# Moving the attention visits of a fused attention + two-layer MLP + top-2 experts kernel to other half steps, and giving the second layer's four PSUM banks tiles of their own

## The chip, the cores and the metric

The kernel runs on one core of one Trainium2 chip. The metric is the device time of one execution in microseconds (us), lower is better. Five engines work side by side on one core: TensorE (PE in the profile, its weight loads PEld), VectorE (DVE), ScalarE (ACT), GpSimd (POOL) and SyncE (SP), the last one used here to issue DMAs. Each engine runs its own list of instructions strictly in the order in which the kernel's Python code emits them; semaphores order the engines among each other and are inserted by the framework from the tiles that an instruction reads and writes.

## The reference, cut to what matters

```
# 1. attention inside chunks of 64 rows, 8 batches x 8 heads x 576 rows x 64 columns
scores = q_c @ k_c.T / 8 ; attn = softmax(scores) ; x = attn @ v_c
x = x.transpose(0, 2, 1, 3).reshape(4608, 512)
# 2. an MLP, 512 -> 2048 -> 512
h = x @ w_in ; x = (h - tanh(h)) @ w_out
# 3. eight experts, two per token, 512 -> 1024 -> 512
noisy = x @ w_gate + log1p(exp(x @ w_noise)) * noise
top2, weights = two largest of noisy, softmax over the two
out[token] = sum over its two experts e of weight * (relu(x @ w1[e]) @ w2[e])
```

## The kernel before

The 4608 tokens are 36 tiles of 128. Eleven groups of 4, 3, 4, 3, 4, 3, 3, 3, 3, 3, 3 tiles (`GS`) go through the MLP, then the eight experts follow, three groups of token slots each. Group g of the MLP has 16 steps, one for each 128 columns of the hidden layer. A step is two blocks on PE: `layer1` (`products1`, line 269, 12 matmuls into the bank `hp`) and, one step later, `layer2` (`products2`, line 341, three matmuls for each tile, added up over the 16 steps in one PSUM bank of `accs` for each tile). Between the two, `activate` has ACT and DVE make the hidden values `gt`. After the last step of a group `store_y` (or `store_o` for the experts) copies the group's banks to SBUF, in turn on ACT and DVE (lines 383 and 385, 669 and 671).

**Half steps.** `advance(s, h)` emits the layer 1 block of a step, then what is listed in `slots[h]`, then the layer 2 block of the step before, then `slots[h + 1]`. So slot number h is a place in every engine's list right behind PE's block number h. A group of the MLP is `H1` = 32 half steps long. A half step of a group with 3 tiles takes PE about 2.1 us, one with 4 tiles about 2.8 us. All other work is put in these slots by `at(h, fn, ...)`; what is listed first in a slot is emitted first.

**Attention visits.** The attention of the tiles of group 0 is done in a prologue, that of the later tiles in visits, `u_attn`, each a piece of three tiles at once: the transposes of the softmax of the middle one (`u_t`), the product with V of the oldest (`p_mm`), the scores of the newest (`s_mm`), then `p_split` of the oldest (ACT and DVE read its product out of PSUM), and `s_max` and `s_sub` of the newest (DVE). The exponential (`u_x`, ACT) and the normalisation (`u_e`, DVE) of the newest follow one and two half steps later. A tile is finished after three visits. `s_mm(i)` and `p_mm(i)` also issue the loads of q, k and v of tile i + 2 on SP. The products of a visit are 64 small matmuls of 64 x 64, line 124, four at a time in quarters of the array. All of them write the tile `pair`, which has two PSUM banks.

**Other users of `pair`.** `misc()` hands out one of the two banks of `pair` to the logits (`u_lg`, line 415), the gates (`u_gate`, line 434) and the positions (`u_pos`, lines 516 and 517) of the group before; in group 0 `decode`, which turns 64 bit weights into 32 bit ones on DVE (lines 243 to 246), uses them too. The prologue's visits use, beside `pair`, the two halves of `accs`, which is one tile of four banks.

**What follows a group of the MLP.** In the next group, `u_z` (half steps 1 on) loads the stored rows again, `u_yt` (5 on, one each half step) transposes them on DVE (line 391), `u_lg` multiplies them with the gate weights at half step 9, or 10 where the group after this one has four tiles, `u_gate` comes two half steps later, `u_gate2` to `u_gate3` follow, `u_pos` comes 14 after `u_lg`. From there on the tokens are scattered: `u_pos` fills the list `waiting`, and `issue(s)`, called after each slot, pops one entry, a reload of a tile (then two indirect DMAs `xs`) or one indirect DMA `lst`, each behind a small POOL copy that waits for a mark of the step (line 318). The indirect DMAs are POOL instructions, line 544. With three tiles they are handed out from half step 23 to 31, with four into the first half steps of the next group.

**Where visits stand before.** Group 0: half steps 3, 8, 13, 21, 29. Later groups: 5, 13, 21, 29 where the next group has four tiles, else 11, 20, 29. The slot of a visit lists it ahead of everything else in that slot.

Of the kernel before, what the change touches and what calls it, by code (L numbers as in the profile page):

```python
# [9 lines left out]
F32 = mybir.dt.float32  # L10
# [7 lines left out]
PSUM = bass.MemoryType.PSUM  # L18
# [12 lines left out]
def moe_chain_kernel(ctx: ExitStack, tc: tile.TileContext, q, k, v, w_in, w_out, wgn, noise,  # L31
                     w1, w2, out):
    nc = tc.nc
    NT = q.shape[0]
    NTOK = NT * 128
    GS = SIZES or [4, 3] * 3 + [3] * ((NT - 21) // 3)
    NG = len(GS)
    G0 = [sum(GS[:g]) for g in range(NG)]
# [10 lines left out]
    pp = ctx.enter_context(tc.tile_pool(name="pp", bufs=1, space=PSUM))  # L49
# [8 lines left out]

    accs = pp.tile([128, 4, 512], F32, name="acc")
    pair = pp.tile([128, 2, 512], F32, name="pair")
    pairs = [accs[:, 0:2], accs[:, 2:4], pair]
    turn = {"acc": 0, "pair": 0, "early": 0}

    def after(what, n):
        turn[what] += 1
        return (turn[what] - 1) % n
# [126 lines left out]
        nc.scalar.copy(hi, px)  # L195
        nc.vector.tensor_tensor(lo, px, hi.bitcast(F32), op=ALU.subtract)  # L196

    def u_attn(i):

        old, mid, new = [t if GS[0] <= t < NT else None for t in (i - 2, i - 1, i)]  # L200
        for t, fn in ((mid, u_t), (old, p_mm), (new, s_mm), (old, p_split), (new, s_max),
                      (new, s_sub)):
            if t:
                fn(t)
# [139 lines left out]

    def new_acc(s):
        if s.f == 0:
            s.grp["acc"] = [accs[:, after("acc", 4)] for _ in s.tiles]

    def finish(s):
        if s.f == s.nf - 1:  # L350
# [2 lines left out]
    def layer2(s):  # L353
        new_acc(s)
        products2(s, len(s.tiles))
        finish(s)
# [408 lines left out]
    def step1(g, f):  # L765
        s = Step()
        s.kind, s.g, s.f, s.nf, s.n = 1, g, f, NF1, 128 * GS[g]
        s.tiles = [128] * GS[g]
        s.A, s.B, s.xt = WI, WO, XT[g]
        s.done = store_y  # L770
        return s
# [3 lines left out]
    def advance(s, h):  # L775
# [10 lines left out]
        if both:  # L786
            new_hp(s)
            new_acc(p)
            where_filled(s, lambda nt: (tail1(nt), tail2(nt)))
            activate(s)  # L790
            finish(p)
        elif s_tail:
            new_hp(s)
            where_filled(s, tail1)
            activate(s)
        elif s:
            layer1(s)
# [4 lines left out]
        if p_tail and not both:  # L802
            new_acc(p)
            where_filled(p, tail2)
            finish(p)
        elif p and not both:
            layer2(p)
# [6 lines left out]
    def L(f, *a):  # L814
        return lambda: f(*a)
# [11 lines left out]
    def decode_w(o, f, early=False):  # L827
        if f < NF1:
            RW[o, f] = decode(RW[o, f], early)
# [67 lines left out]
    rebias_w(1, 1)  # L897
    decode_w(0, 2)

    plans = [EVEN, ODD] if NG % 2 == 0 else [ODD, EVEN]  # L900
    g0 = plans[0][0]
    xt0, xts = {}, {}
# [9 lines left out]
    H1, H2 = 2 * NF1, 2 * NF2  # L912
    slots = [[] for _ in range(H1 * NG + H2 * E * 3 + 2)]

    def at(h, fn, *a):
        slots[h].append(L(fn, *a))

    values = {}
    for g in range(1, NG):
        for j in range(GS[g]):  # L920
            gap = 9 if GS[g] < 4 and g > 1 else 8
            values[G0[g] + j] = H1 * g - 3 - gap * (GS[g] - 1 - j)

    for i in range(GS[0], NT + 2):
        h = values.get(i - 2, 3 + 5 * (i - GS[0]))
        at(h, u_attn, i)
        if i < NT:
            at(h + 1, u_x, i)
            at(h + 2, u_e, i)

    for g in range(NG):
        h0 = H1 * g
        at(h0, load_nz, g)
        if g > 0:
            n = GS[g - 1]
            for j in range(n):
                i = G0[g - 1] + j
                at(h0 + 1 + j, u_z, i)
                at(h0 + 5 + j, u_yt, i)

            h = h0 + (10 if g + 1 < NG and GS[g + 1] > 3 else 9)
            at(h, u_lg, g - 1)
            h += 2
            for d, fn in zip((0, 2, 3, 4, 6, 7, 12), (u_gate, u_gate2, u_gate2a, u_gate2b,
                                                      u_gate2c, u_gate3, u_pos)):
                at(h + d, fn, g - 1)
        if g == 0:
            at(25, sums)
            at(26, store_consts)
            for f in range(NF1):  # L950
                at(2 * f, fetch_w, 0, f + 4)
                at(2 * f, decode_w, 1, f + 1)
                at(2 * f, prep_w, 0, f + 2)
                at(2 * f, rebias_w, 0, f + 3)
                at(2 * f + 1, fetch_w, 1, f + 4)
                at(2 * f + 1, decode_w, 0, f + 3)
                at(2 * f + 1, prep_w, 1, f + 1)
                at(2 * f + 1, rebias_w, 1, f + 2)
        else:
            for f in range(0, NF1):  # L960
                if g == 1:
                    if f < E:
                        at(h0 + 2 * f, zero_x, 2 * f)
                        at(h0 + 2 * f, zero_x, 2 * f + 1)
                elif (g - 2) * NF1 + f < NT + DUMMY // 128:
                    at(h0 + 2 * f, zero_out, (g - 2) * NF1 + f)
        if g == NG - 1:
            at(h0 - 4, u_cum)
            at(h0 - 2, u_bump)
            at(h0 + 12, load_list0)  # L970
            for c in range(min(3, SEAL // 128)):
                at(h0 + 8 + 3 * c, fetch_x, 0, c)
            for c in range(g0[1]):
                at(h0 + min(21 + 4 * c, H1 - 1), first_xt, c)
            for f in range(NF2):
                at(h0 + 2 * f + 7, fetch_e, 0, f)
                at(h0 + 2 * f + 10, prep_e, 0, f)
# [26 lines left out]
    for gi, (e, ge, c0, nt, n) in enumerate(groups):  # L1004
        h0 = H1 * NG + H2 * gi
        if gi == 0:
# [4 lines left out]
            h = h0 + 8 + GS[-1]  # L1011
# [18 lines left out]
    for g in range(NG):  # L1030
        grp = {}
        for f in range(NF1):
            s = step1(g, f)
# [3 lines left out]
    for gi, (e, ge, c0, nt, n) in enumerate(groups):  # L1037
        grp = {}
        for f in range(NF2):
            s = Step()  # L1040
# [60 lines left out]
```

## Time and profile before

| | |
|---|---|
| median of 3 runs | 1868.93 us (1867.94 to 1869.45) |
| the profiled execution | 1868.18 us, of which 1866.2 us are the span from its first to its last instruction |
| mean granted TensorE clock | 0.980 of full speed |
| MLP stage, about | 25 to 1003 us of the span; the last visit is at 926 us |
| experts, about | 1003 to 1855 us |

In the rows below, "[2.75 <-DVE e L144]" behind an instruction means that its engine sat idle for 2.75 us just before it, and that this ended with the DVE instruction of line 144 that writes `e`. "<-issue" means that it waited for nothing that the profile shows. L269 is line 269.

### The profile page before, as it was taken

The numbers are of one execution on the slowest core, as the hardware profiler recorded it, in microseconds if no ns is written. First come the engines' busy times: TensorE is split into PE (matmuls) and PEld (weight loads), VectorE is DVE, ScalarE is ACT, GpSimd is POOL, SyncE is SP. The second block draws the span as 40 slices with busy tenths as digits, with TensorE's granted clock in tenths as the row PEclk, the third lists the DMA queues.
The fourth block names the chain that finished last, engine by engine and source line by source line (L and its number), as shares of the span: only waits on it lengthen the run. The fifth ranks groups of instructions, "written<-read, shape, count | busy, mean of one in ns | idle before, by whom it ended". The sixth has DMA issues, their size and how long they took to land. (4 is left out here: it accounts for less than half of the span.)

```text
span 1866.2 us, 28364 instructions
## 1 busy us (share of the span) xinstructions
PE 1770.8 (95%) x10773; PEld 1511.3 (81%) x10775; DVE 802.1 (43%) x2064; ACT 546.7 (29%) x1105; POOL 490.9 (26%) x749
## 2 busy tenths in 40 slices
PE   6989999999999999998999999999999999999997
PEld 5768777887788888887888888888888888887886
DVE  7875434554344445353455442343334323333321
ACT  4543222332223222222233232232223222232211
POOL 3550303040304020211224532232232212322112
PEclk8999999999999999999999999999999999999999
DMA  6536343552213131222045343443434323433312
GB/s 253 197 107 159 108 102 109 151 153 75 86 63 123 41 111 52 86 74 74 36 125 168 106 109 84 108 96 78 113 73 101 96 58 81 103 98 78 67 23 34
DMA packets 197830, 184.68 MB, mean 99 GB/s; under 512 B 80176, under 2 KB 139568, under 8 KB 197680
## 3 DMA queue, kind: packets, MB, share of 16 engines
q1 hardware_dynamic: 178064, 142.73, 25.2%
q0 software_dynamic: 19328, 39.41, 10.6%
q8 instruction: 96, 1.57, 0.3%
q14 instruction: 54, 0.44, 0.1%
q10 hardware_dynamic: 288, 0.52, 0.1%
HBM read 118.76 MB, written 63.84 MB: 98 GB/s over the span
## 5 line engine op out<-in xcount | busy, mean ns | idle before, releaser
L269 PE MATMUL hp<-xt,wa 128*128 128x384 f32 (+3 forms) x4416 | 904.5, 354 | 1.2 <-ACT xt L195 0.7
L341 PE MATMUL acc<-wb,gt 128*128 128x512 f32 (+1 forms) x3510 | 882.6, 397 | 24.1 <-ACT o L669 10.4
L269 PEld LDWEIGHTS hp<-xt,wa 128*128 128x128 f32 x4416 | 785.8, 192 | 86.9 <-issue 3.1
L341 PEld LDWEIGHTS acc<-wb,gt 128*128 128x128 f32 (+1 forms) x3510 | 651.3, 188 | 168.9 <-ACT o L669 16.0
L300 DVE SCALAR_TENSOR_TENSOR gt<-hp,gt 128x384 fp32r<-128x384 f32 (+2 forms) x192 | 113.3, 590 | 451.0 <-ACT gt L297 438.2
L297 ACT ACTIVATE gt<-hp 128x384 fp32r<-128x384 f32 (+2 forms) x192 | 99.5, 518 | 455.9 <-PE hp L269 405.0
L292 DVE TENSOR_TENSOR g<-hp,g 128x384 f32<-128x384 f32 (+1 forms) x176 | 104.1, 591 | 257.6 <-ACT g L289 254.9
L289 ACT ACTIVATE g<-hp 128x384 f32<-128x384 f32 (+1 forms) x176 | 91.5, 520 | 356.2 <-PE hp L269 330.3
L254 POOL TENSOR_TENSOR wb<-st,wb 128x512 fp32r<-128x512 f32 x64 | 93.4, 1460 | 320.1 <-ACT wb L252 320.1
L318 POOL COPY spacer<-mark 1x1 f32<-1x1 f32 x182 | 45.8, 252 | 401.7 <-DVE mark L313 292.8
L293 ACT CAST gt<-g 128x384 fp32r<-128x384 f32 (+1 forms) x176 | 95.4, 542 | 160.0 <-DVE g L292 127.5
L674 POOL DMA_INDIRECT out_dram<-o,lsa x73 | 119.8, 1641 | 77.9 <-DVE o L671 59.1
L295 DVE TENSOR_TENSOR gt<-g,gt 128x384 fp32r<-128x384 f32 (+1 forms) x160 | 94.9, 593 | 96.1 <-ACT gt L293 87.4
L493 POOL TENSOR_SCALAR r<-d 128x3 f32<-128x3 f32 (+1 forms) x11 | 5.4, 487 | 406.5 <-ACT d L484 406.4
L544 POOL DMA_INDIRECT xs<-yr,row x72 | 71.5, 993 | 32.3 <-issue 25.3
L214 DVE TENSOR_TENSOR xt<-xg,xt 128x512 fp32r<-128x512 f32 x80 | 54.3, 679 | 54.4 <-ACT xt L213 54.4
L213 ACT CAST xt<-xg 128x512 fp32r<-128x512 f32 x80 | 48.8, 610 | 96.1 <-DVE xg L391 88.0
L544 POOL DMA_INDIRECT lst<-pay,row x72 | 70.6, 981 | 22.0 <-issue 21.1
L196 DVE TENSOR_TENSOR xt<-pair,xt 128x512 fp32r<-128x512 f32 x33 | 22.8, 691 | 89.6 <-ACT xt L195 79.7
L391 DVE STREAM_TRANSPOSE xg<-xg 128x512 f32<-128x512 f32 x80 | 56.4, 705 | 0.7 <-DMA xg<-xs 0.7
L124 PE MATMUL pair<-ks,q 64*64 64x64 f32 x1024 | 30.9, 226 | 21.7 <-issue 16.2
L671 DVE TENSOR_SCALAR o<-acc,lsa 128x512 f32<-128x512 f32 (+1 forms) x44 | 33.0, 750 | 39.2 <-PE acc L341 22.5
(194 smaller groups left out, 910.0 us busy)
## 6 DMA issues: line engine op xcount, KB each, us to landing
st<-in_w_dram SPq DMA_DIRECT2D x128, 256.0 KB
xg<-xs SPq DMA_DIRECT2D x320, 64.0 KB
out_dram<-zero SPq DMA_DIRECT2D x40, 256.0 KB
x2d<-y SPq DMA_DIRECT2D x36, 256.0 KB
z<-x2d SPq DMA_DIRECT2D x144, 64.0 KB
yr<-x2d SPq DMA_DIRECT2D x36, 256.0 KB
q<-in_q_dram SPq DMA_DIRECT2D x34, 256.0 KB
v<-in_v_dram SPq DMA_DIRECT2D x34, 256.0 KB
```

The lines of the kernel that those rows point to most:

```text
L254: eng.tensor_tensor(w[:, 1, :], x, w[:, 0, :].bitcast(F32), op=ALU.subtract)
L269: nc.tensor.matmul(s.hp[:, :m], lhsT=w[:, a, d, :], rhs=s.xt[:, b, d, :m], start=(i == 0), stop=(i == 11))
L289: nc.scalar.activation(g, hp[:, :n], AF.Tanh)
L292: nc.vector.tensor_tensor(g, hp[:, :n], g, op=ALU.subtract)
L293: nc.scalar.copy(hi, g)
L295: eng.tensor_tensor(lo, g, hi.bitcast(F32), op=ALU.subtract)
L297: nc.scalar.activation(hi, hp[:, :n], AF.Relu)
L300: nc.vector.scalar_tensor_tensor(lo, hp[:, :n], 0.0, hi.bitcast(F32), op0=ALU.max, op1=ALU.subtract)
L341: nc.tensor.matmul(s.grp["acc"][j][:m], lhsT=s.gt[:, a, j * 128:j * 128 + m], rhs=s.B[s.f][:, b, :], start=(s.f == 0 and i == 0), stop=(s. ...
L391: nc.vector.transpose(out=out.rearrange("p b (g c) -> p g b c", g=4), in_=x.rearrange("p (g b r) -> p g b r", g=4, b=4))
L544: s = nc.gpsimd.indirect_dma_start(out=to, out_offset=bass.IndirectOffsetOnAxis(ap=at, axis=0), in_=src, in_offset=None)
L674: a = nc.gpsimd.indirect_dma_start(out=out, out_offset=bass.IndirectOffsetOnAxis(ap=en[:m, 0:1], axis=0), in_=o[:m], in_offset=None, compu ...
```

## The change

The visits get half steps written out by hand: 3, 8, 13, 19, 25 in group 0, of which the last two take no new tile (so group 0 starts tiles 4 to 6 only, before it started 4 to 8); 2, 5, 9, 15, 18, 21 in group 1; later 5, 9, 15, 20 where the next group has four tiles, else 5, 14, 20, up to group 9. There are 36 visits in place of 34, with the same tiles. `u_lg` and all that hangs on it move from half step 10 to 11 where the next group has four tiles. The four banks of layer 2 are no longer slices of the one tile `accs`: the prologue has two tiles of two banks in a pool `ep`, which is closed after it, and the same four banks then become a ring of four tiles `acc` of one bank each.

```diff
-    accs = pp.tile([128, 4, 512], F32, name="acc")
     pair = pp.tile([128, 2, 512], F32, name="pair")
-    pairs = [accs[:, 0:2], accs[:, 2:4], pair]
-    turn = {"acc": 0, "pair": 0, "early": 0}
+    early = ExitStack()
+    ep = early.enter_context(tc.tile_pool(name="ep", bufs=1, space=PSUM))
+    pairs = [ep.tile([128, 2, 512], F32, name=f"pair{i}") for i in range(2)] + [pair]
+    turn = {"pair": 0, "early": 0}
+    accs = []
...
-    def u_attn(i):
-
-        old, mid, new = [t if GS[0] <= t < NT else None for t in (i - 2, i - 1, i)]
+    def u_attn(old, mid, new):
...
     def new_acc(s):
         if s.f == 0:
-            s.grp["acc"] = [accs[:, after("acc", 4)] for _ in s.tiles]
+            s.grp["acc"] = [accs[0].tile([128, 512], F32, name="acc", bufs=4) for _ in s.tiles]
...
+    early.close()
+    accs.append(ctx.enter_context(tc.tile_pool(name="ap", bufs=1, space=PSUM)))
...
-    values = {}
-    for g in range(1, NG):
-        for j in range(GS[g]):
-            gap = 9 if GS[g] < 4 and g > 1 else 8
-            values[G0[g] + j] = H1 * g - 3 - gap * (GS[g] - 1 - j)
-
-    for i in range(GS[0], NT + 2):
-        h = values.get(i - 2, 3 + 5 * (i - GS[0]))
-        at(h, u_attn, i)
-        if i < NT:
+    visits = [(3, 4), (8, 5), (13, 6), (19, None), (25, None)]
+    n0 = sum(GS[:2])
+    for g in range(1, NG - 1):
+        hs = (2, 5, 9, 15, 18, 21) if g == 1 else (5, 9, 15, 20) if GS[g + 1] > 3 else (5, 14, 20)
+        for h in hs:
+            visits.append((H1 * g + h, n0 if n0 < NT else None))
+            n0 += 1
+    flow = [None, None]
+    for h, i in visits:
+        at(h, u_attn, *flow, i)
+        if i:
             at(h + 1, u_x, i)
             at(h + 2, u_e, i)
+        flow = [flow[1], i]
...
-            h = h0 + (10 if g + 1 < NG and GS[g + 1] > 3 else 9)
+            h = h0 + (11 if g + 1 < NG and GS[g + 1] > 3 else 9)
             at(h, u_lg, g - 1)
```

## Rows read from the trace of the kernel before

**Rows 1.** Part 1 of the page: busy time of each engine, share of the span, instructions.
```profile
PE 1770.8 (95%) x10773; PEld 1511.3 (81%) x10775; DVE 802.1 (43%) x2064; ACT 546.7 (29%) x1105; POOL 490.9 (26%) x749
```

**Rows 2.** Who PE waited for over the whole span: the waiting instruction, what ended the wait, us in total, times, the longest.
```profile
PE pair L434 <- DVE e L144: 19.3, 7, 2.8
PE pair L124 <- issue: 16.2, 31, 1.1
PE pair L124 <- DVE x L246: 12.6, 5, 3.0
PE acc L341 <- ACT o L669: 10.4, 8, 2.2
...
PE acc L341 <- DVE o L671: 4.2, 7, 1.0
...
PE acc L341 <- ACT y L385: 3.4, 2, 2.7
PE acc L124 <- DVE xt L196: 2.3, 1, 2.3
PE acc L341 <- DVE y L383: 1.9, 3, 0.6
```

**Rows 3.** Timeline of PE at a visit with the gates in the same slot, group 8, half step 11: start, us, instruction.
```profile
799.07 0.94 PE L434 MATMUL pair<-summat,ls 128*128 128x16 f32 x6 [2.75 <-DVE e L144]
799.84 3.82 PE L269 MATMUL hp<-xt,wa 128*128 128x384 f32 x12
```

**Rows 4.** Stretches from the first matmul of line 124 of such a visit to the end of the next layer 1 block: window, us, busy us of PE (matmuls), of PEld, DVE, ACT, POOL, granted clock, share of the DMA engines, GB/s. The first, the second and the last of seven; the first two have blocks of 512 columns, the later ones of 384.
```profile
261.60:270.62 9.02, 6.27 (x83) 5.19 (x83) 2.16 (x4) 1.59 (x4) 0.00 (x0) 0.81 0.82 203
445.19:452.58 7.39, 4.64 (x83) 4.02 (x83) 2.16 (x4) 1.59 (x4) 0.00 (x0) 1.00 0.66 177
...
880.50:888.83 8.33, 5.58 (x83) 5.44 (x83) 2.17 (x4) 1.59 (x4) 0.00 (x0) 0.80 0.42 128
```

**Rows 5.** The same columns for stretches from the first matmul of line 124 of a visit to the end of the next layer 1 block, without gates in between. The first is in group 0 (blocks of 512 columns), the second at half step 5 of group 3 (384 columns). The other eight are the visits at half step 29 of groups 1 to 8; those that begin at 320.47 and 502.49 have 512 columns, the others 384.
```profile
76.45:80.41 3.96, 3.96 (x76) 3.39 (x77) 2.04 (x4) 1.77 (x4) 2.42 (x2) 1.00 0.54 155
344.08:347.35 3.27, 3.27 (x77) 3.20 (x77) 1.38 (x3) 1.17 (x2) 0.00 (x0) 1.00 0.62 160
213.81:224.28 10.47, 7.09 (x77) 5.89 (x77) 1.01 (x2) 1.17 (x2) 6.22 (x12) 0.77 0.53 184
320.47:326.61 6.14, 4.75 (x77) 3.78 (x77) 1.98 (x3) 1.17 (x2) 1.59 (x3) 1.00 0.34 98
401.90:405.78 3.88, 3.60 (x77) 3.41 (x77) 0.21 (x1) 1.17 (x2) 2.95 (x7) 1.00 0.69 247
502.49:510.37 7.88, 6.38 (x77) 5.15 (x77) 1.98 (x3) 1.17 (x2) 1.90 (x3) 0.78 0.30 102
588.55:591.84 3.29, 3.29 (x77) 3.22 (x77) 0.00 (x0) 0.59 (x1) 2.22 (x5) 1.00 0.66 212
670.74:680.78 10.04, 6.36 (x77) 5.60 (x77) 1.98 (x3) 1.18 (x2) 4.33 (x7) 0.83 0.34 107
756.16:766.13 9.97, 6.74 (x77) 5.39 (x77) 1.98 (x3) 1.17 (x2) 4.35 (x7) 0.83 0.27 86
841.64:851.56 9.92, 6.66 (x77) 5.33 (x77) 1.98 (x3) 1.18 (x2) 4.32 (x7) 0.83 0.17 55
```

**Rows 6.** Timeline inside the last of these visits, PE and POOL.
```profile
842.16 0.75 PE L124 MATMUL pair<-ks,q 64*64 64x64 f32 x13
...
842.86 0.97 POOL L544 DMA_INDIRECT lst<-pay,row   x1 [0.16 <-issue]
...
843.34 0.33 PE L124 MATMUL pair<-ks,q 64*64 64x64 f32 x4 [0.43 <-issue]
```

**Rows 7.** Timeline at the end of an expert's group of three tiles: the first two of three copies out of the layer 2 banks, and the first layer 2 block of the next group.
```profile
1192.53 0.75 DVE L671 TENSOR_SCALAR o<-acc,lsa 128x512 f32<-128x512 f32 x1 [1.07 <-PE acc L341]
1193.31 0.69 ACT L669 ACTIVATE o<-acc,lsa 128x512 f32<-128x512 f32 x1 [2.41 <-DVE o L671]
...
1194.93 1.86 PE L341 MATMUL acc<-wb,gt 128*128 128x512 f32 x7 [0.97 <-DVE o L671]
```

**Rows 8.** Timeline in the prologue: `p_mm(3)` on PE, which writes the second half of `accs` (`p_split(2)`, which it waits for, reads the first half); the last reader of `accs` in the prologue; the first layer 2 block.
```profile
23.62 1.13 PE L124 MATMUL acc<-pts,wb 64*64 64x64 f32 x32 [2.28 <-DVE xt L196]
...
25.43 0.69 DVE L196 TENSOR_TENSOR xt<-acc,xt 128x512 fp32r<-128x512 f32 x1 [1.87 <-ACT xt L195]
...
33.96 2.25 PE L341 MATMUL acc<-wb,gt 128*128 128x512 f32 x9
```

**Rows 9.** Timeline around a visit at half step 20 of group 8 (a visit at an even half step): the block of PE that follows it, and the last DVE instruction of `u_e`, which makes the softmax that the next visit transposes.
```profile
821.95 2.35 PE L341 MATMUL acc<-wb,gt 128*128 128x512 f32 x9
...
829.80 0.69 DVE L168 TENSOR_TENSOR e<-e,sm 128x512 f32<-128x512 f32 x1
```

**Rows 10.** Timeline in group 5, whose `u_lg` takes four tiles: the logits on PE and the last of the four transposes on DVE.
```profile
535.82 1.34 PE L415 MATMUL pair<-x2t,wg 128*32 128x128 f32 x32
...
535.97 0.71 DVE L391 STREAM_TRANSPOSE x2t<-z 128x512 f32<-128x512 f32 x1
```

**Rows 11.** A stretch at the visit at half step 5 of group 1, with the columns of rows 4.
```profile
155.99:160.00 4.01, 4.01 (x81) 3.81 (x81) 2.13 (x4) 1.67 (x3) 0.00 (x0) 1.00 0.86 213
```

**Rows 12.** Timeline of the end: the first of the last three copies out of the layer 2 banks, and the first of the last three indirect DMAs.
```profile
1855.30 0.75 DVE L671 TENSOR_SCALAR o<-acc,lsa 128x512 f32<-128x512 f32 x1 [2.45 <-PE acc L341]
...
1856.46 1.55 POOL L674 DMA_INDIRECT out_dram<-o,lsa  x1 [24.24 <-DVE o L671]
```

## The prediction

> **What bounds the kernel now.** First the busy shares: PE has 1770.8 us of matmuls in a span of 1866.2, every other engine is below half [rows 1]. So PE sets the time, and a change that adds no matmul work can only move what PE loses: idle time, and blocks that run at the slow one of its two clock levels. Second, PE's waits by cause [rows 2]: 19.3 us are seven waits of the gates for `s_sub` of a visit, 16.2 are gaps inside visits that end with no event ("issue"), 12.6 are visits behind a weight decode in group 0, and 19.9 (10.4 + 4.2 + 3.4 + 1.9) are layer 2 blocks that wait until the last group's banks are copied out. Third, stretches of equal work laid beside each other [rows 4, 5], which catch what the list of waits doesn't: the slow clock and matmuls that trickle.
>
> The sum is made against the profiled execution, 1868.18 us, which is the span plus 1.98 us; the median of the runs is 0.75 above it.
>
> **Gates.** At half step 11 a visit and `u_gate` share a slot and the tile `pair`. PE reaches the gates right behind the visit and stands 2.75 us until DVE has done `p_split`, `s_max` and `s_sub`; the next layer 1 block then takes 3.66 us (799.84 to 803.50) [rows 3]. The second of the seven stretches ran at full clock throughout and lost nothing but the wait: 7.39 - 2.75 = 4.64 us quiet for 512 columns [rows 4]. For 384 columns the quiet value is 0.69 less (3.96 against 3.27 in the two quiet visits of [rows 5]), 3.95. The losses are 9.02 - 4.64 = 4.38, then 2.75, then five of 8.33 - 3.95 = 4.38 (the one with four tiles differs by 0.2): 29.0 us. The granted means of 0.81 and 0.80 in the first and the last [rows 4] say that after the wait part of the stretch ran at 1.2 GHz. After the change the nearest user of `pair` behind a visit is two half steps away (visit 9, logits 11), 4.2 us against the 2.75 that DVE needs. So **-29.0**; bounds 25 and 29.
>
> **Visits among indirect DMAs.** The eight visits at half step 29 with the next block [rows 5] took 10.47, 6.14, 3.88, 7.88, 3.29, 10.04, 9.97 and 9.92 us; quiet is 3.27, or 3.96 where the block has 512 columns. Excess: 7.20 + 2.18 + 0.61 + 3.92 + 0.02 + 6.77 + 6.70 + 6.65 = 34.0 us. Inside the last one PE runs 13 score matmuls, then four in a burst, with gaps, while POOL issues one indirect DMA after another [rows 6]. No semaphore of the profile explains the gaps; what differs from the quiet visit is POOL's load (4.32 us busy against 0.00) [rows 5]. The case against: the fifth of the eight, with POOL busy for 2.22 us, lost nothing. With three tiles the indirect DMAs are over by half step 31, and the new places 5, 14, 20 are clear of them; with four tiles the last is popped at half step 4, so the visits at 5 of groups 2 and 4 stand just behind it. I take **-34.0** and, for these two, +2; bounds 0 and -34, and 0 to +14 (two at the worst price, 6.8).
>
> The Trainium skill says otherwise: "PE and ACT never wait on anyone" (SBUF — State Buffer, Who interferes with whom), meaning contention for SBUF's ports. By that rule POOL's DMAs can't be what held PE up, moving the visits would free nothing, and the sum would be 34 us higher. The eight stretches disagree about the waiting, six of them clearly, though not about the ports.
>
> **The ring of layer 2 banks.** At an expert group's end the copies run one behind the other though they read different banks: DVE 1192.53 to 1193.28, ACT from 1193.31, and the next group's layer 2 block starts at 1194.93 behind the third [rows 7]. That group has three tiles and the ring four banks, so the bank it writes first was free long before: the wait hangs on the tile `accs`, not on the bank. The prologue shows the same: `p_mm(3)` waits 2.28 us for a reader of the other half [rows 8]. With a tile for each bank, the copy of tile j starts when its own matmuls end (the last step is sorted by tile), ACT and DVE run side by side, and PE needs the first bank alone. Of the 19.9 us I take **-18**; two stay, because the longest wait for `y`, 2.7 us [rows 2], is more than three serial copies explain. Bounds 0 (the waits stay as they are) and -19.9. Closing the prologue's pool costs nothing: the first layer 2 block comes at 33.96, the last reader of those banks is done at 26.12 [rows 8]. The prologue's wait of 2.28 goes, and much of it reaches the first block: **-2**, bounds 0 and -2.3. At the end the first of three copies waits for the last matmul (idle 2.45 before it), and POOL's three DMAs follow it [rows 12]: **-1.5**, bounds 0 and -2.4.
>
> **Group 0.** Five visits before and after; the last two are smaller, but each still stands behind a decode on `pair`, so the 12.6 us stay: **0**, bounds 0 and -5 (two mean waits of 2.5).
>
> **What is late next: group 1.** It now has six visits, some three half steps (6.3 us) apart. After a visit at an even half step the softmax is ready at 830.49, which is 8.54 us after PE went on at 821.95 [rows 9]. So the visits at 5 and 21 wait 2.2 us each, in `u_t`, and all of PE behind them. The one at 18, behind an odd half step, has up to one DVE queue's work less: 1.2. That is 5.6 us, and a wait of 2.75 cost a slow block of 1.6 in six of seven cases [rows 4]; two such make 3.2. SP gets three loads more for each of the visits at 2 and 9, where at half step 5 the DMA engines are already 0.86 busy [rows 11]. In sum **+9**, bounds 0 and 20.
>
> **Logits.** In groups 2 and 4 to 9 a visit now stands at half step 5, ahead of the transposes that `u_lg` needs. It puts five DVE instructions of 0.69 us [rows 9] before the last of them, 3.5 us. In group 5, with four tiles, the last transpose already ends at 536.68, inside the logits' own 1.34 us [rows 10]: there PE waits about 2.5, and with a chance of a slow block 3.3. The other six have one transpose less, or longer half steps, and I give four of them 0.2 each. **+4**, bounds 0 and 7 x (3.5 + 1.6) = 36.
>
> No instruction is added on any engine but what two more slots hold; the q, k and v loads on SP are the same ones, moved. The half step by which `u_lg` and the scatters of groups 1 and 3 move later delays the reuse of `y` buffers; it is part of the two us left above.
>
> Sum: -29.0 - 34.0 - 18 - 2 - 1.5 + 2 + 9 + 4 = -69.5; 1868.2 - 69.5 = 1798.7, with the 0.75 of the median 1799.
>
> **The rivals.**
> A. PE isn't held up by the indirect DMAs, and visits trickle wherever they stand. For it: the visit of 3.29 us among them. Against: no visit away from half step 29 trickled in rows 5, at 0.62 DMA share. Time: 1799 + 34 = 1833. Chance 0.11.
> B. The framework orders the ring's tiles as it did the slices; the copies stay serial and PE waits for all. Against: the waits follow the tile in both [rows 7, 8]. Time: 1799 + 18 + 2 + 1.5 = 1820. Chance 0.10.
> C. The dense visits and the transposes cost their upper bounds rather than what I gave: DVE's list is late in group 1, and the logits wait in most groups. 1799 + 11 + about half of the 32 = 1826. Chance 0.13.
> D. Slower than before: visits at 5 run among the loads of `u_z` and starve as those at 29 did, 6.8 us each. From 11 starved visits of 36 on (69.5 / 6.8 = 10.2) the kernel is slower; twelve give 1799 + 82 = 1881. Against: the visits at half step 5 of groups 1 and 3 ran quiet among such loads [rows 5, 11]. Chance 0.04.
> E. None of the new costs shows: 1784. Chance 0.02.
>
> **How the numbers follow.** My forecast holds 0.60, own range 1786 to 1812. The range 1783 to 1826 leaves out A, D and a part of C, some 0.19. A difference of 0.2%, 3.7 us, is about what a measurement of this kernel can tell from none. All cases but D are faster by more than that; 0.02 I keep for no change, as a mixture of A, B and C: faster 0.94, same 0.02, slower 0.04.
>
> **What would show it.** Right: no wait of line 434 for `e`; no "issue" gaps at line 124; DVE and ACT copies of one group overlapping, and the waits of line 341 for `o` and `y` below 3 us together; new waits of line 178 for `e` of line 168 at three places in group 1; one of line 415 in group 5; a mean granted clock of 0.985 or more. Wrong: trickling line 124 at the new half steps (A, D), serial copies (B), or line 178 and 415 above 20 us (C).

## The result, and the profile after

On the chip where the kernel before took 1869.19 us (median of 4 runs), the changed one takes **1784.43 us** (median of 4 runs, 1783.46 to 1787.84): ratio 0.9549, 95% interval 0.9532 to 0.9565. The forecast was 1799 (1783 to 1826): the direction was right, and the gain of 84.8 us is 14.6 more than the 70.2 from that same median to 1799. The profiled execution took 1784.29 us, span 1782.4 after 1866.2.

Later runs fell on other chips and brought what no trace of before could show. On chip 11 (numbers as the results give them) the unchanged kernel before takes 1830.76 us, the changed one 1777.56: ratio 0.9713, interval 0.9698 to 0.9728. On chips 3 and 4 the kernel before takes 1863.81 and 1871.01. (The number of the first chip was not kept; it is called the first chip here.) About 39 of the 84 us between the two spans are a loss that the kernel before doesn't have on chip 11; the gain there is only 31 us smaller, because the changed kernel takes 7.6 us less there too.

Part 1 of the page after; it answers to [rows 1]. PE has 30.7 us less of busy time for the same 10773 matmuls: part of the time of trickling visits and of slow blocks counts as busy.

```profile
PE 1740.1 (98%) x10773; PEld 1492.3 (84%) x10775; DVE 796.6 (45%) x2064; ACT 546.4 (31%) x1105; POOL 491.8 (28%) x749
```

Who PE waited for in the changed kernel: the waiting instruction, what ended the wait, us in total, times, the longest; to be laid beside [rows 2].

```profile
PE pair L126 <- DVE x L246: 11.1, 5, 3.8
PE pt L180 <- DVE e L170: 4.7, 2, 2.7
PE pt L180 <- POOL e L170: 4.1, 2, 2.5
PE pt L180 <- DVE ef L500: 2.1, 1, 2.1
...
PE acc L341 <- issue: 1.5, 1, 1.5
...
PE pair L415 <- DVE x2t L391: 0.9, 2, 0.8
...
PE acc L341 <- ACT y L385: 0.5, 1, 0.5
```

Line 434 is gone, the gaps inside visits are gone, and of the layer 2 blocks' waits for `o` and `y` (19.9 us) 0.5 is left. The wait for the decode stays, and waits of line 180 (178 before) are new in group 1, as forecast; the two of them for POOL stand in the prologue, as before.

Timeline at the end of an expert's group of three tiles in the changed kernel, the answer to [rows 7]: the copies on DVE and ACT, and the blocks on PE.

```profile
1122.86 0.74 DVE L671 TENSOR_SCALAR o<-acc,lsa 128x512 f32<-128x512 f32 x1
1123.30 0.69 ACT L669 ACTIVATE o<-acc,lsa 128x512 f32<-128x512 f32 x1 [0.92 <-PE acc L341]
1123.80 1.63 PE L269 MATMUL hp<-xt,wa 128*128 128x352 f32 x12
...
1124.00 0.75 DVE L671 TENSOR_SCALAR o<-acc,lsa 128x512 f32<-128x512 f32 x1 [0.40 <-PE acc L341]
1125.27 1.79 PE L341 MATMUL acc<-wb,gt 128*128 128x512 f32 x7
```

DVE and ACT overlap (1123.30 lies inside 1122.86 to 1123.60), each copy starts when its own tile's matmuls are done, and line 341 starts without a wait.

Stretches of the changed kernel from the first matmul of a visit to the end of the next block on PE (columns of [rows 4]): the visits of group 6 at 5 and 20 (after the latter the block is one of layer 2).

```profile
583.00:586.29 3.29, 3.29 (x77) 3.22 (x77) 1.41 (x3) 1.17 (x2) 0.00 (x0) 1.00 0.37 112
...
619.67:622.93 3.26, 3.26 (x74) 2.83 (x74) 2.08 (x5) 1.65 (x4) 0.85 (x5) 1.00 0.44 143
```

Both are quiet: full clock, busy time equal to the stretch.

Where the time went, by the starts of the groups' first layer 1 blocks in the timelines (us; each column is one span less another):

| stretch | after less before, first chip | after less before, chip 11 | before: chip 11 less first chip |
|---|---|---|---|
| up to the first layer 1 block | -2.8 | -3.8 | +0.5 |
| group 0 | -5.6 | -6.7 | +0.7 |
| group 1 | +3.5 | +9.1 | -8.0 |
| groups 2, 3 | -6.6, -0.3 | -5.7, +0.3 | -0.9, -0.6 |
| groups 4, 5 | -9.6, -5.0 | -4.4, -4.6 | -5.3, -0.5 |
| groups 6, 7, 8 | -12.4, -11.3, -10.6 | -4.5, -4.5, -4.5 | -9.6, -6.7, -6.6 |
| groups 9, 10 | -4.5, +0.6 | -4.6, -0.3 | 0.0, +0.1 |
| experts | -18.7 | -17.7 | -2.1 |
| tail | -0.5 | -0.9 | +0.5 |
| sum | -83.8 | -52.8 | -38.6 |

The last column is the same program on two chips. Nearly all of its difference, 38.4 of 38.6 us, lies in groups 1 to 8, whose visits at half step 29 stand among the indirect DMAs [rows 5]. Elsewhere the start, group 0 and the tail differ by 0.5 to 0.7 the other way, the first three expert groups by 2.1; from the fourth expert group to the tail the two agree within 0.1 us.

### The profile page after: what moved, and what is told of

The parts are those of the page before. It is cut to its first block, busy times and chain, and to the rows that moved or that the text cites. A ratio compares the mean times of both kernels' runs of the same rounds, so it can differ in the third digit from the quotient of the medians.

```text
span 1782.4 us, 28350 instructions
## 1 busy us (share of the span) xinstructions
PE 1740.1 (98%) x10773; PEld 1492.3 (84%) x10775; DVE 796.6 (45%) x2064; ACT 546.4 (31%) x1105; POOL 491.8 (28%) x749
## 3 DMA queue, kind: packets, MB, share of 16 engines
q0 software_dynamic: 19328, 39.41, 11.1%
## 5 line engine op out<-in xcount | busy, mean ns | idle before, releaser
L269 PE MATMUL hp<-xt,wa 128*128 128x384 f32 (+3 forms) x4416 | 888.8, 350 | 1.4 <-ACT xt L197 1.4
L269 PEld LDWEIGHTS hp<-xt,wa 128*128 128x128 f32 x4416 | 771.2, 189 | 85.0 <-issue 2.2
L544 POOL DMA_INDIRECT xs<-yr,row x72 | 71.5, 993 | 31.3 <-issue 25.4
L254 DVE TENSOR_TENSOR wa<-st,wa 128x512 fp32r<-128x512 f32 x64 | 45.2, 706 | 7.5 <-ACT wa L252 7.4
L252 ACT CAST wa<-st 128x512 fp32r<-128x512 f32 x64 | 39.2, 613 | 6.6 <-DMA st<-in_w_dram 6.6
```

What stands on the lines that cost most here:

```text
L254: eng.tensor_tensor(w[:, 1, :], x, w[:, 0, :].bitcast(F32), op=ALU.subtract)
L269: nc.tensor.matmul(s.hp[:, :m], lhsT=w[:, a, d, :], rhs=s.xt[:, b, d, :m], start=(i == 0), stop=(i == 11))
L544: s = nc.gpsimd.indirect_dma_start(out=to, out_offset=bass.IndirectOffsetOnAxis(ap=at, axis=0), in_=src, in_offset=None)
```

## The experiments

**The ring alone.** The kernel before with the tiles of the layer 2 banks changed as in the change (the first and third hunk and the two lines after the prologue), visits where they were.

> The kernel before with the ring of layer 2 banks and the pool of the prologue alone; all visits where they stood before. My theory (the waits of the layer 2 blocks hang on the one tile of four banks): the experts lose 18.7 us as they do in the changed kernel, the waits for the copies of y in the MLP 5 to 6, the prologue 2.8, the tail 0.5, so 1841 to 1847 us (my sum gave this part 21.5: 1847). The trickling visits and the waits of line 434 stay as long as they were. Rival B (the framework orders the ring as it did the slices): 1869, with serial copies.

Measured on chip 11: 1803.78 us beside 1830.71, ratio 0.9856 (0.9839 to 0.9873): -26.9. My 1841 to 1847 were worked out from 1869, and this chip's level is 38 lower; the difference is the 22 to 28 expected. PE's waits in it (two lines were added ahead, so 434 is 436 here):

```profile
PE pair L436 <- DVE e L146: 19.3, 7, 2.8
PE pair L126 <- DVE x L248: 13.4, 5, 3.8
...
PE acc L343 <- DVE o L673: 0.2, 1, 0.2
```

The gates' 19.3 us are untouched, the waits for `o` and `y` are gone. Rival B falls. A line that should be there is missing: no "issue" gaps in visits, though they stand at half step 29 as before. The run of the unchanged kernel before, below, shows that this goes with the chip.

**The visits alone.** The changed kernel with the four banks as slices of one tile.

```diff
+    accs = pp.tile([128, 4, 512], F32, name="acc")
...
-    pairs = [ep.tile([128, 2, 512], F32, name=f"pair{i}") for i in range(2)] + [pair]
...
+    pairs = [accs[:, 0:2], accs[:, 2:4], pair]
...
-            s.grp["acc"] = [accs[0].tile([128, 512], F32, name="acc", bufs=4) for _ in s.tiles]
+            s.grp["acc"] = [accs[:, after("acc", 4)] for _ in s.tiles]
```

> The changed kernel with the four layer 2 banks as slices of one tile again; the visits at their new half steps. My theory: it gives back what the ring brought, 22 to 28 us, so 1806 to 1812 us, with waits of line 341 for o and y of some 20 us in the list. If the two parts don't add up (the ring also feeds the visits, or the visits hide the ring), it differs from 1869 + 1784 less the time of the ring alone by more than 5. Rival B: 1784.

Measured on chip 11: 1804.77 us, 27.2 above the changed kernel there (1777.56). PE's waits:

```profile
PE acc L339 <- ACT o L667: 11.5, 8, 3.3
...
PE acc L339 <- DVE o L669: 4.2, 7, 1.0
```

The waits for `o` and `y` are back (line 341 is 339 here; those for `y` are 1.3 us). The two halves add up: 26.9 for the ring, 25.9 for the visits (1830.71 - 1804.77), 53.2 for both on that chip. Neither feeds the other beyond some tenths.

**The last visit among the indirect DMAs again.**

```diff
-        hs = (2, 5, 9, 15, 18, 21) if g == 1 else (5, 9, 15, 20) if GS[g + 1] > 3 else (5, 14, 20)
+        hs = (2, 5, 9, 15, 18, 21) if g == 1 else (5, 9, 15, 29) if GS[g + 1] > 3 else (5, 14, 29)
```

> The changed kernel with the last visit of groups 2 to 9 at half step 29 in place of 20, among the indirect DMAs again; all other visits and the ring stay. My theory (a visit trickles where indirect DMAs run): the excess of rows 5 comes back where it was, 2.2 + 0.6 + 3.9 + 0 + 6.8 + 6.7 + 6.65 for groups 2 to 8, so some 27 us: 1811 (1804 to 1816). In group 9, whose last visit does not meet a later one, none. Rival A (the trickle had to do with the neighbours of the visit, not with the indirect DMAs): 1784, and no gaps that end with no event in line 126.

Measured on chip 11: 1781.17 us, 3.6 above the changed kernel there, 2.6 of them in group 1, where the two kernels are the same. The 1811 that I expected did not come; by the words on record this is rival A: no trickle. Stretches from those visits to the end of the next layer 1 block, groups 2 and 7:

```profile
311.03:314.99 3.96, 3.96 (x77) 3.39 (x77) 1.82 (x3) 1.17 (x2) 1.56 (x3) 1.00 0.48 142
...
711.34:714.60 3.26, 3.26 (x77) 3.19 (x77) 1.38 (x3) 1.17 (x2) 2.94 (x5) 1.00 0.60 208
```

POOL is 1.56 to 2.97 us busy in the seven stretches, with indirect DMAs, and nothing is lost. But the kernel before, run beside it, took 1830.71, not 1869. Before believing the rival, the kernel before itself had to be looked at on this chip.

**The kernel before once more**, unchanged.

> The kernel before once more. On the chip of the runs of the ring alone and of the visits at 29 it took 1830.7 us, 38 less than in the runs that I predicted from. My theory now: what is missing there are the 34 us of the visits that trickle among indirect DMAs (rows 5), so the loss belongs to some chips and not to the kernel alone. If this run takes 1867 to 1871, the visits at half step 29 trickle as in rows 5; if 1827 to 1832, all of them take 1.1 to 1.2 us, and the waits of line 434 for e (19.3), of line 341 for o and y (some 20) and for the decode (12.6) are as in rows 2. Rival: the 38 us lie elsewhere, in a higher granted clock or in shorter waits.

Measured on chip 11: 1829.59 us (one run). Four of the eight stretches of [rows 5], the same visits of the same program (groups 1, 4, 6, 8):

```profile
215.12:218.39 3.27, 3.27 (x77) 3.20 (x77) 1.27 (x2) 1.17 (x2) 2.84 (x6) 1.00 0.82 271
...
492.78:496.74 3.96, 3.96 (x77) 3.39 (x77) 1.98 (x3) 1.17 (x2) 1.91 (x3) 1.00 0.45 151
...
653.75:657.04 3.29, 3.29 (x77) 3.22 (x77) 1.29 (x2) 1.17 (x2) 2.96 (x5) 1.00 0.63 213
...
811.16:814.45 3.29, 3.29 (x77) 3.22 (x77) 1.29 (x2) 1.17 (x2) 2.97 (x5) 1.00 0.49 165
```

Quiet to the hundredth: 3.27 where [rows 5] has 10.47, 3.96 for 7.88, 3.29 for 10.04, 3.29 for 9.92. The other waits are nearly the same (gates 19.3 us, line 341 for `o` 9.8 + 4.2), but for one: the 3.4 us of line 341 for ACT's copies of `y` [rows 2] are not listed at all. POOL's side is the same: the 72 indirect DMAs into `lst` have a median of 967 ns, on the first chip 966. So the trickle is not in the program alone.

**The changed kernel once more**, unchanged.

> The changed kernel once more, beside the others of this call. My theory: it loses nothing to trickling visits on any chip, so 1778 to 1785 us wherever it runs, and its gain over the kernel before is 84 us on a chip where visits trickle and 46 to 52 on one where they don't. Rival (the other chip is quicker as a whole): it is 38 us quicker there too, 1746.

Measured beside it on chip 11: 1777.56 us (1776.71 to 1780.23), -53.2. As expected it is nearly the same on both chips; of the 7.6 us between the two spans 2.5 lie in group 1, 1.8 in group 6 (one "issue" wait of line 341, 1.48 us, at 576.52 on the first chip), the rest in pieces of about 1.

**The middle visit back beside the gates.**

```diff
-        hs = (2, 5, 9, 15, 18, 21) if g == 1 else (5, 9, 15, 20) if GS[g + 1] > 3 else (5, 14, 20)
+        hs = (2, 5, 9, 15, 18, 21) if g == 1 else (5, 9, 15, 20) if GS[g + 1] > 3 else (5, 11, 20)
```

> The changed kernel with the middle visit at half step 11 in place of 14 in the groups that had it at 14, so that it shares a slot with the gates and with the tile pair again. My theory: in each group in which a visit with new scores meets the gates there, 4.4 us (2.75 of wait for DVE and 1.6 of slow clock behind it), seven or fewer of them: 1784 + 22 to 31 = 1806 to 1815. Where only the wait comes back and no slow clock, 1784 + 2.75 x 7 = 1803. A rival: DVE's list is shorter than before and the wait shrinks to 1 or below: 1791 or less.

Measured on chip 11: 1811.73 us, 34.2 above the changed kernel there. By group: 4.4 in group 2, 6.0 and 5.8 in groups 4 and 5, 4.4 in each of 6 to 8, 1.5 in group 9, together 30.8; the rest is mostly group 1 (2.5 us of slow blocks), where this kernel does the same as the changed one. PE's waits, and the gates of one group (the wait, then the layer 1 block that follows):

```profile
PE pair L434 <- DVE e L146: 16.5, 6, 2.8
...
PE pair L434 <- DVE xt L198: 1.4, 1, 1.4
```
```profile
616.38 0.84 PE L434 MATMUL pair<-summat,ls 128*128 128x16 f32 x6 [2.76 <-DVE e L146]
617.07 3.64 PE L269 MATMUL hp<-xt,wa 128*128 128x384 f32 x12
```

The wait and a slow block come back with the place (2.76 and 3.64 here, 2.75 and 3.82 in [rows 3]). The gates' term holds.

**Without the indirect DMAs into `lst`.** The kernel before with a small POOL memset in the place of each, groups 0 to 8.

```diff
-                waiting.append(L(scatter, lst, row[:, 1, c:c + 1], pay[:, j, kk, :], "entries"))
+                if g >= NG - 2:
+                    waiting.append(L(scatter, lst, row[:, 1, c:c + 1], pay[:, j, kk, :], "entries"))
+                else:
+                    waiting.append(L(nc.gpsimd.memset, spacer, 0.0))
```

> The kernel before without the indirect DMAs that write the list entries (lst) of groups 0 to 8, a small POOL memset in the place of each; it leaves out that scatter, so most tokens are missing in the output. On a chip where visits trickle: the five visits of rows 5 that met lst (3.9 + 2.2 + 6.8 + 6.7 + 6.65 = 26 us) run quiet, 1843, and those that met xs (213.81 and 401.90) stay as they were; by rival A 1869. On a chip where they don't: 1827 to 1832, no change.

Measured on chip 11: 1831.65 beside 1830.76, ratio 1.0006 (0.9996 to 1.0016): nothing to gain where nothing trickles. Later the same kernel ran on chip 4:

> The kernel before without the indirect DMAs that write lst in groups 0 to 8 once more, in the hope of a chip on which visits trickle (it leaves out that scatter, so most tokens are missing in the output). If the kernel before takes 1860 to 1870 beside it: by my theory the visits at half step 29 that met lst, of groups 2, 4, 6, 7 and 8 (26 us in rows 5), run quiet, so 24 to 30 us less than the kernel before, while those of groups 1 and 3 that met xs trickle on. Rival (the transfers of q, k and v or POOL's marks hold PE up, not the indirect DMAs): within 3 us of the kernel before. If the kernel before takes 1830 it tells nothing new.

Measured there: 1842.44 us beside 1871.01, ratio 0.9847 (0.9813 to 0.9881): -28.6. The stretches that answer to [rows 5], groups 1 to 6 (7 and 8 are as 6, 3.27 and 3.29):

```profile
213.55:224.44 10.89, 7.31 (x78) 6.11 (x78) 1.98 (x3) 1.17 (x2) 5.33 (x12) 0.70 0.65 198
319.86:323.82 3.96, 3.96 (x77) 3.39 (x77) 1.98 (x3) 1.17 (x2) 0.05 (x1) 1.00 0.52 170
399.14:403.02 3.88, 3.58 (x77) 3.38 (x77) 0.00 (x0) 0.69 (x2) 2.96 (x7) 1.00 0.71 248
499.85:503.81 3.96, 3.96 (x77) 3.38 (x77) 1.98 (x3) 1.17 (x2) 0.06 (x1) 1.00 0.52 170
583.35:586.96 3.61, 3.47 (x77) 3.20 (x77) 0.00 (x0) 0.58 (x1) 2.55 (x8) 1.00 0.65 225
664.60:667.89 3.29, 3.29 (x77) 3.22 (x77) 1.41 (x3) 1.17 (x2) 0.61 (x5) 1.00 0.62 211
```

The five that had met `lst` are quiet now; the three that meet `xs`, left in place, are not (10.89, 3.88, 3.61). Same half step, same loads of q, k and v, same POOL copies: what went is the indirect DMAs. On a chip that shows the trickle they cause it; whether it is POOL's instruction or the transfer that it starts, this run doesn't separate.

**The last visit at 29 on a chip that trickles.** The kernel of the last experiment below (five tiles in group 0), with and without the visit at 29 in place of 20; its edit is the one that put the last visit at 29 above.

> The same with the last visit of groups 2 to 9 at half step 29 in place of 20, among the indirect DMAs. On a chip where the kernel before takes 1830 us and no visit trickles: the same time within 2 us (the visits at 29 cost nothing there, as in the first run of that place). On a chip where it takes 1869: 25 to 30 us more than the same kernel with that visit at 20, in visits of 3 to 7 us at half step 29.

Measured on chip 3: 1812.26 us, with that visit at 20 it is 1780.94: +31.3. The stretch of group 8:

```profile
810.00:820.37 10.37, 7.13 (x78) 5.88 (x78) 1.98 (x3) 1.18 (x2) 4.34 (x7) 0.74 0.17 53
```

The same edit that cost nothing at half step 29 on chip 11 costs 31.3 us here, the 25 to 30 that I expected and a little more. Over all seven stretches the excess is 27.0 us; the groups themselves lose 31.1: some 4 us fall after the next layer 1 block, outside the window that I had measured. In group 5, for one, PE waits 1.59 us for ACT behind it.

**Six visits in group 1 spread out.**

```diff
-        hs = (2, 5, 9, 15, 18, 21) if g == 1 else (5, 9, 15, 20) if GS[g + 1] > 3 else (5, 14, 20)
+        hs = (1, 5, 9, 15, 19, 23) if g == 1 else (5, 9, 15, 20) if GS[g + 1] > 3 else (5, 14, 20)
```

> The changed kernel with the six visits of group 1 at half steps 1, 5, 9, 15, 19, 23 in place of 2, 5, 9, 15, 18, 21, so that each has four half steps or more before the next. My theory: the three waits of line 180 in group 1 (2.05, 2.70, 2.14) and the slow blocks behind them go, 7 to 10 us less than the changed kernel: 1775 where that takes 1784. Rival (DVE's list is late for another reason, or the visit at 23 meets the first indirect DMAs): no change within 2 us.

Measured on chip 11: 1770.96 us (1769.54 to 1773.03), 6.6 below the changed kernel beside it. Line 180's waits for DVE in group 1 fall from 7.4 us (the changed kernel on chip 11) to 0.6, none for `ef`; in the profiled executions group 1 itself is 6.4 us shorter, group 0 1.5 longer. This version beats both kernels on chip 11; on chip 3, in the next experiment, the same group 1 takes 0.5 us more, so that the visit at 23 doesn't trickle there either.

**Decode's words in SBUF**, on top of that.

```diff
-            part = bank().bitcast(U32)
+            part = sp.tile([128, 512], U32, name="word", tag="ls", bufs=1)
```

> The visits of group 1 at 1, 5, 9, 15, 19, 23 (1771.0 us on this chip) and, on top, decode's intermediate words in a tile of SBUF rather than in a bank of pair. My theory: the five visits of group 0 stand behind the decode only because both use pair; their 11.9 us of waits for line 246 go, and 2 to 4 us of slow blocks behind them: 1755 to 1759. Rival (DVE is what is late in group 0, and whatever a visit needs of it comes as late): the waits move to other lines of the visit, and the time falls by less than 4: 1767 to 1771.

Measured on chip 3: 1781.65 us (the kernel before 1863.81). Another chip, so the totals can't be laid beside 1771; group 0, which no indirect DMA touches and which differs by 0.3 to 0.7 us between the first chip and chip 11 for one and the same kernel, can: it is 7.3 us longer than without this edit. My theory falls, and the rival's small gain did not come either. PE's largest wait in this kernel, then one step of the decode in group 0, first on DVE and then, over the same time, on POOL:

```profile
PE hp L269 <- DVE mark L313: 9.3, 3, 3.8
```
```profile
102.31 0.69 DVE L244 SCALAR_TENSOR_TENSOR word<-wb,word 128x512 uint32<-128x512 uint32 x1
103.04 1.67 DVE L246 SCALAR_TENSOR_TENSOR x<-wb,word 128x512 uint32<-128x512 uint32 x1
...
102.66 1.50 POOL L295 TENSOR_TENSOR gt<-g,gt 128x512 fp32r<-128x512 f32 x1 [2.68 <-ACT gt L293]
```

The visits no longer wait for line 246, but the work on DVE got slower: with both inputs in SBUF an instruction of this form takes 1.67 us when POOL's `tensor_tensor` has begun before it, 0.69 where it begins before POOL (the rows at 103.04 and 102.31, two lines of one form). Of line 246's thirty instances in group 0 fifteen take 1.56 to 1.68 us, each begun while a `tensor_tensor` of POOL ran, and the other fifteen 0.69, with none beside them; with the words in a bank of `pair` none took over 0.70. PE waits behind DVE elsewhere. The Trainium skill has the rule (SBUF — State Buffer, Who interferes with whom): a DVE instruction with two SBUF inputs contends with a GpSimd instruction that reads SBUF. The trace agrees, 1.67 against 0.69; the bank in PSUM was what kept them apart.

**Five tiles in group 0 again**, four visits in group 1, on top of that.

```diff
-    visits = [(3, 4), (8, 5), (13, 6), (19, None), (25, None)]
-    n0 = sum(GS[:2])
+    visits = [(3, 4), (8, 5), (13, 6), (19, 7), (25, 8)]
+    n0 = sum(GS[:2]) + 2
...
-        hs = (1, 5, 9, 15, 19, 23) if g == 1 else (5, 9, 15, 20) if GS[g + 1] > 3 else (5, 14, 20)
+        hs = (3, 9, 15, 21) if g == 1 else (5, 9, 15, 20) if GS[g + 1] > 3 else (5, 14, 20)
```

> The kernel with decode's words in SBUF and, on top, five tiles started in group 0 again (4 to 8, at 3, 8, 13, 19, 25) and only four visits in group 1 (3, 9, 15, 21), as many tiles as before by the end of group 1. My theory: group 1 has six half steps between visits, so no wait of line 180 for the softmax is left there; 1 to 4 us less than with decode's words in SBUF alone. Rival (three more loads for each of two more tiles in group 0 come late among the weight loads, or DVE's list grows beyond the half steps there): up to 6 us more.

Measured on chip 3: 1780.94 beside 1781.65, no difference and neither of the two expected: group 0 gets 2.2 us longer, group 1 1.6 shorter, the rest is a few tenths. Moving two visits' work between the two groups is worth nothing.

## Why the prediction came out as it did

The order of the terms was right, and the named signs are in the trace (mean granted clock 0.991; of the three waits of line 180 in group 1 two are for `e`, one for the group's `ef`); the point lay 14 us too high because most unknowns were taken at the cautious side and several terms were sized by the idle time that the profile lists.

There is luck in it too. The result lies 1.4 us inside the lower edge of the range, and it comes from the chip that the rows were read on. On chip 11 the same change ends at 1777.56, below the range, with a gain of 53.2 us; nothing in rows 1 to 12 could have told the two apart.

- **Gates, -29.0.** Right in mechanism, 1.8 beyond the bound of 29. Putting the visit back gives 30.8 us in the six groups and group 9, with the same wait and slow blocks behind it. (The block of [rows 3] takes 3.82 us, as its row says; the forecast's 3.66 runs to the start of the next one. The sum doesn't use it.)
- **Visits among indirect DMAs, -34.0, and +2 for those at 5 of groups 2 and 4.** Right in kind and place for the chip that I had a trace of, and too small: the same kernel loses 38.4 us in groups 1 to 8 there against chip 11 (the table's last column). The step that was too narrow is the window: I summed PE's time to the end of the next layer 1 block, and looked at PE alone. The visit of group 5, which I put at 0.02 and held for the case against, was not spared. ACT's copy of its product starts 4.58 us after PE is done with it, on chip 11 0.87 (the first chip, then chip 11):

```profile
593.82 0.59 ACT L195 CAST xt<-pair 128x512 fp32r<-128x512 f32 x1 [4.58 <-remote]
```
```profile
576.53 0.59 ACT L195 CAST xt<-pair 128x512 fp32r<-128x512 f32 x1 [0.87 <-PE pair L124]
```

  ("remote", like "issue", names no instruction of this profile.) ACT is late from there on, PE waits 1.60 us for `gt` at the start of group 6, and 2.9 us are lost there. At the start of group 4, behind the visit of group 3, it is 3.0 us, PE's longest wait for `y`:

```profile
418.45 3.04 PE L341 MATMUL acc<-wb,gt 128*128 128x512 f32 x12 [2.73 <-ACT y L385]
```

  ACT's copy, line 385, starts 3.54 us after PE's last matmul into the bank there, on chip 11 0.03 us after. Without the indirect DMAs into `lst`, on chip 4, line 195 starts 0.53 us behind PE in groups 2, 4, 6, 7 and 8. (In groups 2 and 4 chip 11 has 1.2 and 1.6 us more of slow blocks behind the gates, so the loss itself is nearer 41 than 38.4.) What I could not see is that this term differs from chip to chip: rival A's claim (PE isn't held up by the indirect DMAs) holds on chip 11 and fails on the first chip, 3 and 4. The residue of 2 at the two visits is about 0.2 (4.03 and 4.12 us in the stretches from 238.97 and 412.75 of the changed kernel, quiet 3.96), but there is that one wait of 1.48 at 576.52.
- **The ring, -18 - 2 - 1.5.** The mechanism is shown by two experiments; the size is 27, mis-sized by 5.5. I had taken the idle that [rows 2] lists, and 14.6 us listed in the experts were worth 18.7 (17.7 on chip 11, where 14.0 are listed). One group's end shows it: from layer 1 block to layer 1 block over the waiting block the kernel before takes 1196.63 - 1192.33 = 4.30 us, the changed one 1126.90 - 1123.80 = 3.10 us, a difference of 1.20 for a wait listed as 0.97 [rows 7]. The rows of before that aren't shown above, and the one of after that follows the fence at the group's end:

```profile
1192.33 1.63 PE L269 MATMUL hp<-xt,wa 128*128 128x352 f32 x12
...
1196.63 1.63 PE L269 MATMUL hp<-xt,wa 128*128 128x352 f32 x12
```
```profile
1126.90 1.27 PE L269 MATMUL hp<-xt,wa 128*128 128x352 f32 x9
```

  The prologue gave 2.8 (4.4 with the ring alone on chip 11), the tail 0.5 to 0.9 instead of 1.5, and the two us that I left standing for `y` were 0.5: the wait of 2.7 us that made me leave them is the late ACT shown above; on chip 11 the same copies, one behind the other, are done before PE needs the banks.
- **Group 0, 0.** Failed, and beyond its bound of -5: -5.6, on chip 11 -6.7. The waits for the decode stayed (11.1 of 12.6), as said, but I had asked only after the waits. Groups 0 and 1 of the kernel before on chip 11, then of the changed one beside it (columns of [rows 4]):

```profile
25.98:142.55 116.57, 102.11 (x644) 81.32 (x645) 93.81 (x155) 59.00 (x105) 59.37 (x47) 0.93 0.42 142
142.55:220.49 77.94, 77.30 (x655) 68.62 (x653) 42.50 (x127) 24.94 (x53) 12.81 (x36) 1.00 0.52 147
```
```profile
22.17:132.09 109.92, 96.74 (x576) 76.42 (x577) 88.25 (x148) 57.77 (x102) 59.75 (x48) 0.97 0.44 155
132.09:219.08 86.99, 79.58 (x723) 69.88 (x721) 48.45 (x139) 26.74 (x56) 10.89 (x33) 1.00 0.51 146
```

  PE does 68 matmuls fewer in group 0 and 68 more in group 1, where they cost 79.58 - 77.30 = 2.3 us. Group 0's busy time falls by 5.4; the 3.1 beyond these matmuls go with a granted clock of 0.97 in place of 0.93. Its idle time (the stretch less PE's busy time) falls by 14.5 - 13.2 = 1.3. Why the clock is higher there, no run was made to show.
- **Group 1, +9.** Right in sum, +9.1 on chip 11, by other parts: in the rows above idle rises by 7.4 - 0.6 = 6.8 (5.6 forecast), 2.3 is the work moved from group 0, which I had not counted, and the slow blocks (3.2 forecast) are missing at a clock of 1.00; on the first chip, where the old trickle of 8.0 goes as well, there are 2.5 us of them. That is not the chip: the two kernels above with a visit at 29 and at 11 have the same group 1 and show them on chip 11 too, at a clock of 0.96. The three waits are where I put them (behind the visits at 2, 15 and 18, so in those at 5, 18 and 21), and the one at 18, put at 1.2 us, is the longest. In the changed kernel on the first chip:

```profile
149.19 0.66 PE L180 MATMUL pt<-ident,e 128*128 128x128 f32 x4 [2.05 <-DVE e L170]
...
187.64 1.12 PE L180 MATMUL pt<-ident,e 128*128 128x128 f32 x4 [2.70 <-DVE e L170]
...
199.50 0.63 PE L180 MATMUL pt<-ident,e 128*128 128x128 f32 x4 [2.14 <-DVE ef L500]
```

  That spreading the visits by one or two half steps takes 6.4 us away confirms their cause: the softmax needs 8.54 us behind a visit [rows 9], and three half steps are 6.3.
- **Logits, +4.** Too high: one wait of 0.78 us in group 5 (2.5 forecast) and 0.1 elsewhere. The DVE list had more slack there than the sum of its instructions suggested.

What the terms gave beyond the forecast: ring 5.5, visits 4.4, group 0 5.6, gates 1.8, logits 3.1, together 20.4. Against them stand the 7.6 us that the changed kernel takes more on the first chip than on chip 11, of which I had allowed 2. 20.4 - 5.6 = 14.8, beside the 14.3 of the spans (83.8 less the forecast 69.5); the ring and group 0 share about a us, and gates and ring were measured on chip 11.

Of the rivals, A holds on chip 11 alone, B falls with the ring alone, C and D with the waits after. The time of E came out, but not its reason: the new costs of group 1 are there in full, and larger gains paid for them.

## What to carry to other kernels

A loss for which the profile names no releaser may differ from chip to chip: run the unchanged kernel on another one before costing its removal, and give the gain for both (85 and 53 us here). Look for such idle on every engine: a visit that PE got through unhurt had made ACT late. A wait hangs on what the framework orders as one tile, so give each bank that is freed by itself a tile of its own; and size a PE wait by laying the stretch beside a quiet one, which gave 1.2 us for a listed 0.97. Before moving an intermediate out of PSUM to be rid of an ordering, look who else reads SBUF at that time.

## What was not expected of the hardware

On chips 3 and 4 and the first chip PE is held up during back-to-back indirect DMAs of POOL, on chip 11 it isn't, with the same program. That it is the chip, and not the time of the run, is likely but not shown: only chip 11 is known to have been used at two times, and it was quiet at both. Timeline of PE inside the first such visit on chip 4 (the kernel without `lst`):

```profile
214.07 0.39 PE L124 MATMUL pair<-ks,q 64*64 64x64 f32 x10
214.86 0.31 PE L124 MATMUL pair<-ks,q 64*64 64x64 f32 x3 [0.40 <-issue]
215.60 0.35 PE L124 MATMUL pair<-ks,q 64*64 64x64 f32 x6 [0.43 <-issue]
216.35 0.37 PE L124 MATMUL pair<-ks,q 64*64 64x64 f32 x5 [0.40 <-issue]
```

PE runs a few matmuls every 0.74 to 0.79 us (214.07, 214.86, 215.60, 216.35), a beat that POOL's issues, 1.3 to 1.5 us apart, don't have.

PE is not alone. Idle of ACT and DVE that no instruction of the profile ends, in the kernel before on the first chip (the largest of each):

```profile
ACT xt L195 <- remote: 12.7, 2, 8.1
...
DVE gt L300 <- issue: 12.4, 4, 4.9
```

In all it is 37.7 us on ACT and 34.6 on DVE, and in the changed kernel there still 24.8 and 54.1, nearly all of it beside indirect DMAs (the whole idle counts, so a part is ordinary waiting). In the eight traces of chip 11 there is none on ACT and a single one of 0.2 us on DVE. So the change takes PE's dense pieces out of the way of the effect; the effect stays, where little of PE's time hangs on it.

Which part of the chip sets the beat, and why chip 11 is free of it, stays open: the indirect DMAs take as long there (median 967 ns). By the sentence of the Trainium skill weighed in the prediction, "PE and ACT never wait on anyone" (SBUF — State Buffer, Who interferes with whom), chip 11 is the rule and the others the exception; the runs don't show that ports have to do with it.
